# Sliding-window attention and an MLP on one core: which queue brings the first tiles' q and k, how the layer norm's weight arrives, and where the sinks' product is made

## The chip, the cores and the metric

The kernel runs on one core of a Trainium2 chip. The core has a matrix engine (TensorE, PE in the profile; its weight loads are PEld), a vector engine (VectorE, DVE), an activation engine (ScalarE, ACT), a general engine (GpSimd, POOL), a sync engine (SyncE, SP) that issues transfers, and 16 DMA engines that all queues share. SyncE and ScalarE issue transfers to hardware queues. GpSimd issues them to a software queue; in this kernel the loads on it are changed from float32 to bf16 on the way, and those on the hardware queues are not.

The metric is the device time of one execution in microseconds (us), lower is better.

## The reference

Attention with a sliding window of 128 and 4 sink positions over 4 batches, 8 heads, 768 positions and 64 dimensions a head, then a layer norm, a two-layer MLP with ReLU, and a residual:

```python
scores = scale * np.matmul(q, k.transpose(0, 1, 3, 2))
keep = (pos[None, :] < n_sink) | ((rel >= 0) & (rel < window))   # rel = query - key
a = softmax(np.where(keep, scores, -1e9))
x = np.matmul(a, v)                       # heads side by side: [4, 768, 512]
xn = (x - mean) / np.sqrt(var + 1e-6) * g_ln
out = x + np.maximum(xn @ w_ch1, 0.0) @ w_ch2     # 512 -> 2048 -> 512
```

All inputs and the output are float32 in memory.

## The kernel before, in words

The 3072 rows (4 batches of 768) are cut into 24 tiles of 128 rows, and these into 12 chunks of two tiles. For a tile, q, k and v are brought in as 128 rows by 8 heads by 64, in bf16. q and k are transposed, so that the head dimension lies on the partitions. TensorE makes the scores of a tile with itself and with the tile before. ScalarE takes the exponential, a mask is applied, and TensorE multiplies with v, to which a column of ones is appended so that the softmax's sum comes out as a 65th column. From the third tile of a batch on, the four sink positions are outside the window; their part comes from `kts` (the sinks' k) and `vs` (the sinks' v, laid out by head). VectorE divides (L793, L795), and takes the layer norm's mean and variance (L799, L801); x minus its mean is transposed on TensorE (L816) and multiplied with the layer norm's weight `gt` on the way out of PSUM (L827). GpSimd makes the inverse standard deviation (L808, L809). The MLP's first layer is L849 (L842 for the first chunk, which goes tile by tile), ReLU is L859 or L861, the second layer L878, the residual L886, the store L890. The first-layer weights `w1` come in four loads of 512 columns (L520), the second-layer weights `w2` in four loads of 512 rows (L523).

Nothing here is in the order of the program text. Each piece of work is given to a planner (`Plan.op`) with the engines that can do it, an estimate of its duration, a priority (lower goes first), and what it reads and writes. `Plan.run` plays the schedule through with these estimates, also for the transfers, and fixes for each engine the order of its work. Every engine then works through its own list in order; a piece that waits for its input holds up all that stands behind it in that list. `nb` is a time before which the planner does not start a piece. `HW_F`, `SW`, `SW_W` and the like are the planner's figures for a transfer (its occupation of the DMA engines, the time before it and the time after it). Where the planner sees a hole in TensorE's list in the first 24 us, the program fills it with matmuls on a tile of zeros (L944). Transfers from GpSimd's queue rotate over eight semaphores, so that the ninth waits until the first has landed; the hardware queues have eight likewise.

The start, which the change touches:

- Chunk 0 (tiles 0 and 1): k comes by SyncE's queue and q by ScalarE's, in float32, each as two loads of 256 KB (four heads by 256 rows, L570). Two neighbouring rows go to one partition, so that each piece is 512 bytes long. Each load is cast to bf16 (L574, on ScalarE or VectorE), and transposed by four matmuls with an identity, whose results are interleaved as float32 in PSUM (L582), and copied out (L553).
- Chunk 1 (tiles 2 and 3): k and q come by GpSimd's queue with the cast, one load a tile (L599), and are transposed by L604 and copied out as bf16 (L553). v comes by GpSimd's queue for all tiles (L547).
- GpSimd's list begins with two selects that make the identity and the triangle (L458, L461). Then come k2, v0, q2, v1, k3, q3, the first w1 load, v2, v3, three w1 loads, and the loads of chunk 2 and of w2.
- `gt` is one load on SyncE's queue that gathers 512 single float32 values (L504). `vc`, the sinks' v, is eight small loads on SyncE's queue (L508). `vs` of batch 0 is made from it on VectorE (L512), not before 12 us in the plan.
- The masks that are multiplied into the exponentials of tile 3 and later (L479, L480) are built on VectorE at about 3.7 us; tiles 0 to 2 get their mask by a matmul that adds a large negative number (L671).

Of the kernel before, what the change touches and what calls it, by code (L numbers as in the profile page):

```python
# [211 lines left out]
def fix(occ, extra=0.09):  # L212
# [5 lines left out]
HW_F = (0.8, 2.2, 0.5)  # L218
# [10 lines left out]
           w1p=(1.6, 2.6, 2.7, 2.8), pm=3, w2p=(4.5, 4.51, 4.52, 4.53), apart=2, by_tile=1, vp=(0.0, 0.1, 2.0, 2.1, 4.55, 4.56), ld1=0.05)  # L229
# [135 lines left out]
def kernel(  # L365
# [43 lines left out]
    ring("natc", 4, [128, 2, 4, 64], BF16)  # L409
# [24 lines left out]
    gt = const("gt", [128, NDM], FP32)  # L434
# [14 lines left out]

    def constant(name, eng, us, prio, emit, reads=(), **kw):  # L450
        return P.op(name, {eng: fix(us)}, prio, emit, reads=[Bc[r] for r in reads], **kw)
# [6 lines left out]
    constant("idf1", "POOL", 0.3, -99, lambda e: G.affine_select(  # L458
        out=ident_f, in_=ident_f, compare_op=ALU.not_equal, fill=1.0, base=0,
        pattern=[[-1, 128]], channel_multiplier=1), rw=[Bc["ident_f"]])  # L460
    constant("up1", "POOL", 0.3, -98, lambda e: G.affine_select(  # L461
# [27 lines left out]
    def negs(e):  # L489
# [3 lines left out]
    constant("negs", "DVE", 0.9, -55, negs, ["upper"], writes=[Bc["neg"]])  # L493
# [8 lines left out]
    constant("masks", "DVE", 0.8, 6.0 if PAR["pm"] == 4 else -20.0, masks, ["upper"], writes=[Bc["mask"]], nb=20.0 if PAR["pm"] == 4 else 0.0)  # L502

    P.op("gt", {"SP": (0.4, 0.4)}, 3.0, lambda e: nc.sync.dma_start(gt, moe_g_ln.rearrange("(j p) -> p j", p=128)),  # L504
         writes=[Bc["gt"]], dma=HW_T)
    for h in range(H):
        p0 = 32 * (h // 2) + NS * (h % 2)
        P.op(f"vcd{h}", {"SP": (0.3, 0.3)}, 3.2 + 0.01 * h, lambda e, h=h, p0=p0: nc.sync.dma_start(  # L508
            vc[p0:p0 + NS, :, 0:64], v[:, h, 0:NS, :].rearrange("b s d -> s b d")),
            reads=[Bc["vc"]], writes=[Bc["vcd"]], dma=HW_T)  # L510
    for b in range(B):
        P.op(f"vs{b}", {"DVE": dve(520)}, 2.0 if b == 0 else 48.0 * b - 20, lambda e, b=b: V.tensor_tensor(  # L512
            vs[b], vc[:, b, :].unsqueeze(1).to_broadcast([128, H, 65]),
            sel.unsqueeze(2).to_broadcast([128, H, 65]), op=ALU.mult),
            reads=[Bc["vcd"], Bc["vc"], Bc["sel"]], writes=[Bvs[b]], nb=12.0 if b == 0 else 40.0 * b)

    w1prio = PAR["w1p"]
    for c in range(4):
        sl = slice(512 * c, 512 * (c + 1))
        P.op(f"w1ld{c}", {"POOL": (0.75, 0.8)}, w1prio[c], lambda e, c=c, sl=sl: G.dma_start(  # L520
# [15 lines left out]

    def early(t):
        return 0.5 + 0.8 * t
# [17 lines left out]
    def chunk(c):  # L556
# [3 lines left out]
        if c < 2:  # L560
            kT_b[c], qT_b[c] = Buf(f"kT{c}", "kT"), Buf(f"qT{c}", "qT")
            if c == 0:
                nats = [Buf("kf", "natf"), Buf("qf", "natf")]
                for hh in range(2):
                    hs = slice(4 * hh, 4 * hh + 4)
                    for i, (x, T) in enumerate(((k, kT_b[c]), (q, qT_b[c]))):
                        nm, src, part = "kq"[i], nats[i], Buf(f"{'kq'[i]}l{hh}")
                        ap = x[b, hs, 0:256, :].rearrange("h (p i) d -> p h (i d)", i=2)
                        P.op(f"{nm}ld{hh}", {("SP" if i == 0 else "ACT"): (0.53, 0.53)}, -70 + hh,
                             lambda e, src=src, ap=ap, hs=hs: (nc.sync if e == "SP" else nc.scalar).dma_start(  # L570
                                 src.t[:, hs].rearrange("p h i d -> p h (i d)"), ap), writes=[src, part], dma=HW_F)
                        nat, pt, done = Buf(f"{nm}c{hh}", "natc"), Buf(f"pt{nm}{hh}", "one"), Buf(f"{nm}T0{hh}")
                        P.op(f"cast{nm}{hh}", {"DVE": dve(512), "ACT": act(512)}, d + 0.01 * hh,
                             lambda e, nat=nat, src=src, hs=hs: (nc.scalar.copy if e == "ACT" else V.tensor_copy)(  # L574
                                 nat.t, src.t[:, hs].rearrange("p h i d -> p i h d")),
                             reads=[part], hold=[src], writes=[nat])

                        def tr(e, pt=pt, nat=nat):
                            pb = pt.t.rearrange("p (h m i) -> p h m i", h=2, i=2)
                            for hp in range(2):  # L580
                                for i in range(2):
                                    nc.tensor.matmul(pb[:, hp, :, i], lhsT=nat.t[:, i, 2 * hp:2 * hp + 2, :], rhs=ident,  # L582
                                                     start=hp + i == 0, stop=True, skip_group_check=True)
                        o = P.op(f"tr{nm}{hh}", pe(0.3), d + 0.02 + 0.01 * hh, tr, reads=[nat, Bc["ident"]], hold=[T], writes=[pt])
                        trs[0], trs[1] = trs.get(0, [o]), [o]
                        evict(f"ev{nm}0{hh}", d + 0.05 + 0.01 * hh, 512,
                              lambda pt=pt: pt.t.rearrange("p (h c) -> p h c", h=2),
                              lambda T=T, hh=hh: T.t[:, 2 * hh:2 * hh + 2, :], [pt], [T, done], fp=True)
                        for t in range(2):
                            tile_of[nm, t, hh] = done  # L590
# [397 lines left out]
```

## Time and profile before

| what | value |
|---|---|
| runs of the kernel before | 220.88, 221.36, 221.38 us (median 221.36) |
| the profiled execution | 221.36 us, its span 219.9 us |
| TensorE | busy 212.3 us of the span, 2033 matmuls |
| VectorE, ScalarE, GpSimd | busy 118.1, 108.8, 89.5 us |
| GpSimd's queue | 13.11 MB in 74944 packets |
| hardware queues (q1, q10) | 13.93 MB in 33600 packets |

The span runs from the first instruction to the last; the rest of the time lies around it. A line such as L582 is a line of the kernel's text. In a table by stretch each engine's busy time is followed by the number of its instructions in brackets, then come the granted share of TensorE's clock, the DMA engines' busy share and the GB/s moved. In a DMA table a queue's line gives packets, megabytes and the share of 16 engines that its packets took; shares over 100% mean that packets overlap. GpSimd's queue is `q0`, SyncE's and ScalarE's are `q1` and `q10`. "DMA to landing" gives least, median and greatest time from the start of an issue until all of the transfer has arrived.

### The profile page before, as it was taken

How to read it: one execution, taken by the hardware profiler on the slowest of the kernel's cores; microseconds unless marked ns; L12 is line 12 of the kernel's file. 1: busy time of each engine (PE TensorE's matmuls, PEld its weight loads, DVE VectorE, ACT ScalarE, POOL GpSimd, SP SyncE). 2: the span in 40 equal slices, each digit the busy share in tenths (PEclk: the TensorE clock that was granted, in tenths of full speed). 3: DMA queues.
4: the chain of work that ended last, by engine and by line, in shares of the span. 5: the costliest groups of instructions: out<-in, count | busy, mean ns of one | idle time of the engine just before them, and what ended most of it. 6: DMA issues, size and time to landing. Idle time of an engine off the chain costs nothing.

```text
span 219.9 us, 5071 instructions
## 1 busy us (share of the span) xinstructions
PE 212.3 (97%) x2033; PEld 144.7 (66%) x2033; DVE 118.1 (54%) x269; ACT 108.8 (49%) x163; POOL 89.5 (41%) x130
## 2 busy tenths in 40 slices
PE   6898999999999999999999999999999999999993
PEld 2566975764965964964955964964965964965852
DVE  5499745585797735735715815725716715732011
ACT  3776564145546447445546447445546447440610
POOL 7987663798065570760442722740110110120000
PEclk9999999999999999999999999999999999999999
DMA  5999999999999997999999999998723521121103
GB/s 158 158 183 207 176 206 196 155 211 155 162 176 152 138 143 114 148 132 119 143 101 142 127 116 130 135 132 107 124 48 75 125 45 48 48 51 48 48 12 101
DMA packets 108574, 27.44 MB, mean 125 GB/s; under 512 B 99200, under 2 KB 105600, under 8 KB 108544
## 3 DMA queue, kind: packets, MB, share of 16 engines
q0 software_dynamic: 74944, 13.11, 83.1%
q1 hardware_dynamic: 32544, 13.41, 29.4%
q10 hardware_dynamic: 1056, 0.52, 0.9%
q8 instruction: 18, 0.29, 0.6%
q14 instruction: 12, 0.10, 0.1%
HBM read 27.30 MB, written 6.29 MB: 153 GB/s over the span
## 4 chain that ended last, share of the span: by engine, by line
PE 91%; DVE 4%; DMA 2%; ACT 1%; issue 1%; DVEq 0%
PE one L878 39%; PE one L849 35%; PE pair L732 5%; PE pair L780 4%; PE one L842 2%; DMA natf<-in_k_dram 2%; PE pair L775 1%; DVE st L799 1%; PE one L638 1%; DVE x L795 1%; PE one L582 1%; PE one L736 1%; PE pair L671 1%; DVE xnt L827 1%; PE one L816 0%
## 5 line engine op out<-in xcount | busy, mean ns | idle before, releaser
L878 PE MATMUL one<-w,h 128*128 128x512 bf16 (+1 forms) x400 | 89.0, 371 | 0.0
L859 ACT ACTIVATE h<-one 128x512 bf16<-128x512 f32 x95 | 56.8, 598 | 59.5 <-PE one L849 54.2
L849 PE MATMUL one<-xnt,w 128*128 128x256 bf16 x704 | 82.4, 273 | 0.0
L849 PEld LDWEIGHTS <-w 128*128 128x128 bf16 x704 | 67.5, 98 | 10.1
L878 PEld LDWEIGHTS <-h 128*128 128x128 bf16 x400 | 37.4, 98 | 38.6 <-issue 2.1
L750 DVE TENSOR_TENSOR pe<-pe,mask 128x1024 bf16<-128x1024 bf16 (+1 forms) x40 | 26.0, 649 | 54.5 <-ACT pe L746 53.6
L746 ACT ACTIVATE pe<-pair 128x1024 bf16<-128x1024 f32 (+1 forms) x40 | 36.2, 957 | 34.1 <-PE pair L732 34.1
L624 POOL DMA_DIRECT2D nat<-in_k_dram x16 | 14.2, 891 | 37.8 <-DMA kT<-nat 24.3
L886 DVE SCALAR_TENSOR_TENSOR ot<-one,st,x 128x512 f32<-128x512 f32 (+1 forms) x25 | 18.1, 726 | 15.3 <-PE one L878 15.2
L808 POOL TENSOR_SCALAR st<-st 128x1 f32<-128x1 f32 x24 | 6.9, 289 | 42.5 <-DVE st L801 41.3
L547 POOL DMA_DIRECT2D vn<-in_v_dram x24 | 21.9, 916 | 3.7 <-DMA w<-in_moe_w_ch_dram 3.0
L624 POOL DMA_DIRECT2D nat<-in_q_dram x16 | 14.6, 913 | 13.4 <-DMA qT<-nat 12.0
L799 DVE BATCH_NORM_STATS2 st<-x 128x6 f32<-128x512 bf16 x24 | 16.7, 694 | 0.8
L809 POOL TENSOR_TENSOR st<-st,mhalf 128x1 f32<-128x1 f32 x24 | 14.8, 618 | 2.0
L780 PEld LDWEIGHTS <-pe 128*128 128x128 bf16 x352 | 14.0, 97 | 2.2 <-ACT pe L691 0.6
L795 DVE TENSOR_TENSOR x<-pair,rec 128x512 bf16<-128x512 f32 x20 | 13.8, 691 | 0.7
L732 PEld LDWEIGHTS <-kT 64*128 64x128 bf16 x216 | 6.9, 94 | 8.5 <-issue 8.3
L780 PE MATMUL pair<-vn,pe 128*128 128x65 bf16 x296 | 12.2, 193 | 0.0
L732 PE MATMUL pair<-qT,kT 64*128 64x128 bf16 (+1 forms) x216 | 11.6, 238 | 0.0
L803 DVE TENSOR_SCALAR xc<-x,st 128x512 bf16<-128x512 bf16 x24 | 9.6, 402 | 0.9
L793 DVE RECIPROCAL rec<-pair 128x8 f32<-128x8 f32 x20 | 4.0, 200 | 9.9 <-PE pair L780 9.9
L691 ACT ACTIVATE pe<-pair 128x1024 bf16<-128x1024 f32 (+1 forms) x8 | 7.2, 918 | 3.3 <-PE pair L685 3.3
(84 smaller groups left out, 123.9 us busy)
## 6 DMA issues: line engine op xcount, KB each, us to landing
out_dram<-ot SPq DMA_DIRECT2D x23, 256.0 KB
w<-in_moe_w_ch_dram POOLq DMA_DIRECT2D x8, 512.0 KB, 12.8
vn<-in_v_dram POOLq DMA_DIRECT2D x24, 128.0 KB, 6.4
nat<-in_k_dram POOLq DMA_DIRECT2D x22, 128.0 KB, 5.8
nat<-in_q_dram POOLq DMA_DIRECT2D x22, 128.0 KB, 5.3
natf<-in_q_dram ACTq DMA_DIRECT2D x2, 256.0 KB
natf<-in_k_dram SPq DMA_DIRECT2D x2, 256.0 KB
xnt<-xc SPq DMA_TRANSPOSE x18
```

The costliest lines, as they stand in the source:

```text
L547: P.op(f"vld{t}", {"POOL": (0.87, 0.9)}, prio, lambda e: G.dma_start(bv.t[:, :, 0:64], v[b, :, 128 * r:128 * (r + 1), :].rearrange("h p d ...
L624: lambda e, nat=nat, ap=ap: G.dma_start(nat.t, ap), writes=[nat], dma=SW)
L732: nc.tensor.matmul(pp.t[:, h2, col:col + q1 - q0], lhsT=kt.t[rs, hp, k0:k0 + 128], rhs=qT.t[rs, hp, q0:q1], start=i == 0, stop=True, skip_ ...
L746: P.op(f"ex{c}{hp}", {"ACT": act(2 * n)}, d + 0.1 + 0.05 * j, lambda e, pp=pp, pb=pb: nc.scalar.activation(pb.t[:, :, 0:n], pp.t[:, :, 0:n ...
L750: V.tensor_mul(pb.t[:, :, 0:n], pb.t[:, :, 0:n], mm),
L780: nc.tensor.matmul(bank(h // 4)[:, 65 * (h % 4):65 * (h % 4) + 65], lhsT=part(h, n), rhs=vn_b[tv].t[:, h, :], start=(not R and h % 4 == 0 ...
L795: P.op(f"x{t}{run[0]}", {"DVE": dve(512 * share)}, dd + 0.11, lambda e, pv=pv, rc=rc, run=run: V.tensor_tensor(x.t[:, 256 * run[0]:256 * r ...
L799: P.op(f"bn{t}", {"DVE": fix(0.60)}, d + 0.12, lambda e: V.bn_stats(st.t[:, 8:14], x.t), reads=[x], writes=[st, mv])
L849: nc.tensor.matmul(ph.t[:, 256 * s:256 * s + 256], lhsT=w1[ht // 4][:, j, 128 * (ht % 4):128 * (ht % 4 + 1)], rhs=xnt.t[:, j, :], start=j ...
L859: nc.scalar.activation(hb.t, ph.t, AF.Relu)
L878: nc.tensor.matmul(pc.t[:, 0:wd], lhsT=(h1[2 * s + i].t[:, 128 * ii:128 * ii + 128] if by_tile else h1[ht // 2].t[:, 256 * (ht % 2) + 128 ...
L886: V.scalar_tensor_tensor(ot.t[:, sl], in0=pc.t[:, 0:wd], scalar=st.t[:, 16:17], in1=x.t[:, sl], op0=ALU.mult, op1=ALU.add),
```

## The change

- Of the first tiles' q and k, only k of tile 0 still comes by the hardware queues: 128 rows in two loads of 128 KB, heads 0 to 3 by SyncE's queue, heads 4 to 7 by ScalarE's, each cast in a piece of 256 elements. q of tile 0, and k and q of tile 1, come by GpSimd's queue with the cast, as those of tiles 2 and 3 do. All four tiles are transposed in the same way, four transposes an operand into bf16 in PSUM. The ring `natc` goes.
- GpSimd's work at the start gets priorities by one list, `front`: q0, the identity, the triangle, k1, q1, v0, v1, k2, q2, the first w1 load, v2, k3, q3, v3, `vs` of batch 0, and the three other w1 loads.
- `vs` of batch 0 is made on GpSimd. Those of the other batches stay on VectorE.
- The layer norm's weight comes as four rows of 128 values, is transposed by TensorE, and copied to `gt` by VectorE.
- The multiplied masks are built not before 5.4 us in the plan. The planner's figures for the first hardware loads, for the sinks' small loads and for the transposes change.

```diff
-HW_F = (0.8, 2.2, 0.5)
+HW_F = (0.5, 0.8, 0.7)
...
-           w1p=(1.6, 2.6, 2.7, 2.8), pm=3, w2p=(4.5, 4.51, 4.52, 4.53), apart=2, by_tile=1, vp=(0.0, 0.1, 2.0, 2.1, 4.55, 4.56), ld1=0.05)
+           pm=3, w2p=(4.5, 4.51, 4.52, 4.53), apart=2, nbs=(0.0, 5.4), by_tile=1, hw=("k0",),
+           front=("q0", "ident", "upper", "k1", "q1", "v0", "v1", "k2", "q2", "w0", "v2", "k3", "q3", "v3", "vs", "w1", "w2", "w3"))
...
+    def early(t):
+        return 0.5 + 0.8 * t
+
+    def front(name):
+        return -110.0 + 0.1 * PAR["front"].index(name)
...
-    constant("idf1", "POOL", 0.3, -99, lambda e: G.affine_select(
+    constant("idf1", "POOL", 0.3, front("ident"), lambda e: G.affine_select(
...
-    constant("masks", "DVE", 0.8, 6.0 if PAR["pm"] == 4 else -20.0, masks, ["upper"], writes=[Bc["mask"]], nb=20.0 if PAR["pm"] == 4 else 0.0)
-
-    P.op("gt", {"SP": (0.4, 0.4)}, 3.0, lambda e: nc.sync.dma_start(gt, moe_g_ln.rearrange("(j p) -> p j", p=128)),
-         writes=[Bc["gt"]], dma=HW_T)
+    constant("masks", "DVE", 0.8, 6.0 if PAR["pm"] == 4 else -20.0, masks, ["upper"], writes=[Bc["mask"]], nb=20.0 if PAR["pm"] == 4 else PAR["nbs"][1])
+
+    g_rows, ptg = Buf("g_rows"), Buf("ptg", "one")
+    P.op("gtld", {"SP": (0.4, 0.4)}, 3.0, lambda e: nc.sync.dma_start(g4, moe_g_ln.rearrange("(j p) -> j p", p=128)),
+         writes=[g_rows], dma=HW_T)
+    P.op("gttr", pe(0.1), early(0) + 0.3, lambda e: nc.tensor.transpose(ptg.t[:, 0:NDM], g4, ident_f[0:NDM, 0:NDM]),
+         reads=[g_rows, Bc["ident_f"]], writes=[ptg])
+    P.op("gtev", {"DVE": fix(0.08)}, early(0) + 0.5, lambda e: V.tensor_copy(gt, ptg.t[:, 0:NDM]), reads=[ptg], writes=[Bc["gt"]])
...
-        P.op(f"vs{b}", {"DVE": dve(520)}, 2.0 if b == 0 else 48.0 * b - 20, lambda e, b=b: V.tensor_tensor(
+        P.op(f"vs{b}", {"DVE": dve(520)} if b else {"POOL": (0.9, 1.0)}, front("vs") if b == 0 else 48.0 * b - 20, lambda e, b=b: (V if b else G).tensor_tensor(
...
-        P.op(f"w1ld{c}", {"POOL": (0.75, 0.8)}, w1prio[c], lambda e, c=c, sl=sl: G.dma_start(
+        P.op(f"w1ld{c}", {"POOL": (0.75, 0.8)}, front(f"w{c}"), lambda e, c=c, sl=sl: G.dma_start(
...
+            for t in (2 * c, 2 * c + 1):
                 d, at_t = early(t), slice(128 * (t % 2), 128 * (t % 2) + 128)
+                shared = Buf(f"pt{t}", "one") if c else None
+                for i, (x, T) in enumerate(((k, kT_b[c]), (q, qT_b[c]))):
+                    nm, nat = f"{'kq'[i]}{t}", Buf(f"{'kq'[i]}n{t}", "nat")
+                    ap = x[b, :, 128 * t:128 * t + 128, :].rearrange("h p d -> p h d")
+                    if nm in PAR["hw"]:
+                        src = Buf(f"{nm}f", "natf")
...
                         for hh in range(2):
+                            hs, part = slice(4 * hh, 4 * hh + 4), Buf(f"{nm}l{hh}")
+                            P.op(f"{nm}ld{hh}", {("SP", "ACT")[hh]: (0.5, 0.5)}, -70 + i,
+                                 lambda e, raw=raw, ap=ap, hs=hs: (nc.sync if e == "SP" else nc.scalar).dma_start(
+                                     raw()[:, hs], ap[:, hs]), writes=[src, part], dma=HW_F)
...
+                    else:
+                        P.op(f"{nm}ld", {"POOL": (0.87, 0.9)}, front(nm), lambda e, nat=nat, ap=ap: G.dma_start(nat.t, ap),
+                             writes=[nat], dma=SW)
```

## The prediction

> **What bounds the kernel now.** I read the page's busy shares first, then the busy time by stretch, the chain of waits of the first 30 us, and last the loads. All times are microseconds from the start of the span.
>
> ```profile
> PE 212.3 (97%) x2033; PEld 144.7 (66%) x2033; DVE 118.1 (54%) x269; ACT 108.8 (49%) x163; POOL 89.5 (41%) x130
> ...
> 5.46:8.00 2.54, 2.47 (x20) 1.66 (x21) 0.90 (x2) 2.05 (x4) 2.54 (x4) 1.00 1.77 162
> 8.00:12.00 4.00, 3.50 (x53) 2.31 (x52) 2.65 (x8) 2.64 (x5) 4.00 (x6) 1.00 2.32 159
> 12.00:16.00 4.00, 3.67 (x56) 2.27 (x54) 3.79 (x10) 3.11 (x5) 3.15 (x6) 1.00 1.71 186
> 16.00:20.00 4.00, 3.50 (x68) 2.80 (x65) 3.79 (x11) 2.95 (x7) 3.04 (x5) 1.00 1.31 206
> 20.00:22.60 2.60, 2.08 (x40) 1.72 (x38) 2.53 (x7) 1.36 (x3) 2.03 (x3) 1.00 1.24 207
> 42.00:216.00 174.00, 174.00 (x1584) 118.56 (x1580) 90.82 (x190) 84.57 (x126) 59.78 (x87) 1.00 1.06 112
> ```
>
> After the stretch come its length, then the busy time of PE, PEld, DVE, ACT and POOL. From 42 to 216 TensorE is never idle at a granted clock of 1.00: nothing in this change can shorten that part. TensorE's loss is 5.46 us before its first useful matmul, and 0.07 + 0.50 + 0.33 + 0.50 + 0.52 = 1.9 us of gaps up to 22.6. What the change can win or lose is there.
>
> ```profile
> 1.02 3.75 DMA natf<-in_k_dram
> 4.79 0.63 ACT natc L574
> ...
> 12.30 0.70 DVE st L799
> ...
> 16.68 0.70 DVE vs L512
> ...
> 22.82 2.68 PE one L842 x48
> ```
>
> The chain (start, length, what): the first k load, its cast, ACT's exponentials, then VectorE from 11 to 21 (busy 3.79 of 4 us), the sinks' product at 16.68 among it; from 21.6 TensorE itself.
>
> ```profile
> q10 hardware_dynamic: 857, 0.43, 66.7%
> q1 hardware_dynamic: 722, 0.33, 50.0%
> ...
> q0 software_dynamic: 1681, 0.21, 166.8%
> ...
> DMA to landing us min/median/max: 6.2/6.3/6.5
> ...
> DMA to landing us min/median/max: 8.0/11.0/13.7
> ...
> DMA to landing us min/median/max: 3.5/6.4/13.4
> ```
>
> The first two lines are all the DMA traffic of 3.6 to 6.0, and the third is GpSimd's queue from 6 to 8: its first load, issued at 1.86, moves nothing until the hardware queues' 1 MB is through. The landings are those of the tile 2 and 3 loads (L599), of w1 (L520), and of v (L547). The four w1 loads are issued at 7.36 and 9.84 to 12.1; the first lands at 7.36 + 8.0 = 15.4, and TensorE's first L842 starts at 15.43; the last, issued at 11.33, lands 13.7 later, at 25.0, and the L842 group that needs it starts at 25.56. So two things bound the front together: VectorE's chain, and a stream of loads that arrives 0.1 to 0.6 us before its use.
>
> **The change part by part.** The profiled execution took 221.36 us, of which 219.9 is the span; it is itself the median of the runs, so the sum is made against 221.36. 0.3% of it, 0.66 us, is about what a measurement tells from no change.
>
> Hardware queues: 1 MB in four loads becomes 256 KB in two, half on SP, half on ACT, both issued at 1.02. The old first half (256 KB) landed 3.75 later. By 3.6 some 0.25 MB had moved, as much as there is now in all; so the new halves land between 3.6 and 4.8. The casts go from four of 512 elements (615 ns on ACT, 448 on VectorE) to two of half that, side by side, about 0.3 us: first useful matmul at 4.1 to 5.2 rather than 5.46.
>
> GpSimd's queue: three loads (q0, k1, q1) are added at 0.9 us of issue each (L599: 0.92 to 1.10). By the new order q0 goes ahead of the two mask selects (0.29 us each), from 1.05 to 2.15. These then end near 2.65 rather than 1.9. That is hidden: their first reader is the transpose of k0 at 4.1. If the cover were gone it would cost 0.75. After them follow k1, q1, v0, v1, k2, q2, the first w1, v2, k3, q3, v3, the sinks' product, and the other w1. With 0.91 each, q2 is issued at 7.2, the first w1 at 8.1, v3 at 11.6.
>
> When do they land? An undisturbed load of this kind lands 3.5 after its issue (least of L547); behind 1 MB it took 6.5. With a quarter of the hardware traffic I take q0 near the first: 1.05 + 3.6 = 4.7, other end 7.55. The last w1, two ways: from q0's landing, the old stream took from k2's landing at 1.86 + 6.5 = 8.4 to 25.0, that is 16.6, for seven small and four large loads; three more small ones at 0.89 give 4.7 + 19.3 = 24.0. By issue, q2 lands at 7.2 + 3.5 = 10.7, and the old spacings (2.56 for w1, 0.98 for each of four small, 7.67 for three w1) give 24.8. I take 24.5: half a microsecond earlier than 25.0 although three loads were added, because the stream starts when it is issued and not at 6.2.
>
> [...]
>
> Transposes: sixteen L582 matmuls at 0.45 to 0.61 us a group of four become sixteen like L604, 0.39 a group. That takes off 0.2 to 0.8 of TensorE time and turns float evictions (0.59 to 0.69) into bf16 ones (0.42 to 0.58). It helps only where TensorE doesn't wait for a load.
>
> Sinks' product: VectorE loses 0.70 that stood on the chain at 16.68. On GpSimd its price isn't in the trace. By rows it lies between 0.7 (VectorE's own) and 1.8 (a 128 element select of 0.29, times 4.06, times the 1.5 by which L809 grew from 0.57 to 0.86 beside a busy VectorE); I take 1.2, by the select. It waits for the eight sink loads, the last of which should be issued near 6.3; even 6.3 us later (L599) they are there at 12.6, about when v3's issue ends. The three w1 are queued behind it; issued at 13.8 rather than 12.5, they still meet a stream busy until 16 to 16.6, so 0. The cover ends when the product ends after 14.7, from where each microsecond costs one. [...]
>
> LN weight: 512 elements of 4 bytes become four rows, a transpose (0.1, as one of L816) and a copy (0.2, as L793 on a small operand). The transpose stands early in TensorE's order, and what lies behind it waits if the rows are late. Their load is issued at 1.5; they come between 3.75 (the first k) and 6.3 (L599) later, at 5.3 to 7.8. I take 5.3, since they follow only k0 on their queue. At 7.8 tile 0 would lose up to 2.5, of which the wait for the first w1 (13.0) still hides most, since tile 0 is otherwise ready near 12.5. Building the masks later (0.32 + 0.27) moves into a VectorE that is busy 1.08 of 4 us there: 0, or 0.6 of the same slack.
>
> Tiles 0 to 3: tile 0's value product moves from 10.5 to about 8.2 (v0 is issued at 4.5 and lands near 8.0), tile 1 with it. k3 and q3 land at 15 to 16 instead of 12 to 13, still ahead of tile 3's old scores at 18.2. So VectorE's chain runs 1 to 3 us ahead and leaves the bound to the loads.
>
> Sum at the last w1, where both kernels meet: landing 0.5 earlier, the 0.56 of slack before its use gone as well, and one second-chunk unit (0.87, L849) that may now run before it, counted at 0.15: 1.2 us. From there on the loads keep their 0.5 lead and TensorE is full. 221.36 - 1.2 = **220.2 us**; its own range, from 0.2 to 0.9 of lead and none or one unit, is 219.5 to 220.7.
>
> **The rivals.** (1) The transfers come no earlier: the added loads use up the earlier start, and the last w1 stays at 25.0. Only slack is won, 0.5: 220.9 (220.7 to 221.5). For it: the bytes are the same and the packets shorter; against it, the undisturbed landing of 3.5.
>
> (2) Slower: GpSimd's first load starts 4.3 after its issue whatever else runs, as k2 did (1.86 to 6.2). Then q0 lands at 7.55 and the last w1 at 7.55 + 19.3 = 26.9, 1.9 later; less 0.56 of slack and none or one unit of 0.87, TensorE loses 0.5 to 1.4: 221.9 to 222.8. It decides once q0 lands after about 6.5. Against it: the hardware queues' traffic ends at the moment GpSimd's begins.
>
> (3) Slower by the sinks' product: it ends after 14.7 and holds three w1 back; ending at 17 it costs 2.3 less 1.1: 222.5.
>
> (4) More is won: TensorE fills the wait for the last w1 with one or two units and saves the 0.8 of transposes: 2.1 to 2.7, so 218.7 to 219.3.
>
> **How the numbers follow.** Forecast 0.47, rival 1 0.20, rival 2 0.15, rival 3 0.08, rival 4 0.10. Below 220.7 lie the forecast but 0.02, rival 4, and 0.04 of rival 1: 0.59. Above 222.02 lie 0.13 of rival 2 and rival 3: 0.21. Between: 0.20. The range 219.2 to 222.5 leaves out most of rival 4 and the upper ends of 2 and 3, together 0.19.
>
> **What would show it.** Right: GpSimd's first packets before 4, q0's landing 3.5 to 4 after issue, the first L842 near 13, the last w1 landing at 24 to 24.8, first useful matmul at or before 5.2, no VectorE product at 16.68. Wrong: packets of GpSimd's queue first at 5 or later, TensorE waiting for the transposed weight, the product ending after 14.7, or gaps of TensorE after 26 that before did not have.

## The result, and the profile after

The changed kernel is slower. Its six runs took 222.68 to 225.07 us, median 223.92; six runs of the kernel before on the same chip took 220.88 to 221.85, median 221.38. The ratio is 1.0099, 95% interval 1.0076 to 1.0123. The profiled execution took 223.05 us with a span of 221.4, so 1.7 us more than the one before; it is one of the quicker of the six. The forecast was 220.2, with a range of 219.2 to 222.5: wrong in sign, and outside the range.

First the busy shares of the changed kernel's page, and its busy time by the same stretches as before (PE, PEld, DVE, ACT, POOL, then the granted clock, the DMA share, GB/s):

```profile
PE 209.6 (95%) x2012; PEld 143.8 (65%) x2032; DVE 116.1 (52%) x267; ACT 108.7 (49%) x163; POOL 92.3 (42%) x134
...
5.46:8.00 2.54, 1.62 (x18) 0.88 (x18) 1.64 (x7) 1.29 (x3) 2.54 (x4) 1.00 1.94 126
8.00:12.00 4.00, 3.08 (x44) 1.69 (x44) 2.72 (x9) 2.11 (x3) 4.00 (x6) 1.00 2.02 146
12.00:16.00 4.00, 2.98 (x48) 1.98 (x49) 3.34 (x9) 2.79 (x6) 3.99 (x5) 1.00 1.76 172
16.00:20.00 4.00, 3.54 (x66) 3.09 (x63) 2.85 (x8) 2.61 (x5) 3.81 (x6) 1.00 1.72 190
20.00:22.60 2.60, 2.35 (x41) 1.73 (x38) 1.70 (x4) 2.26 (x4) 1.39 (x3) 1.00 1.24 208
42.00:216.00 174.00, 172.42 (x1573) 118.53 (x1590) 91.57 (x191) 84.57 (x126) 60.42 (x88) 1.00 1.07 113
```

From 42 to 216 TensorE is as dense as before (20 fewer matmuls than weight loads are in the records of the page, so a few matmuls are missing from it, not from the work). The loss lies ahead of that. VectorE, which was busy 3.79 of 4 us from 12 to 20, now has 3.34 and 2.85: it is no longer the bound. TensorE has more gaps than before from 5.46 to 16 (7.68 of 10.54 us busy, before 9.64). So VectorE and TensorE both wait, and the next view says for what. It is the chain of waits of the first 36 us (start, length, what):

```profile
1.57 1.08 POOL nat L586
...
2.76 0.31 POOL ident_f L464
3.06 0.24 POOL upper L467
3.31 1.74 POOL nat L586 x2
...
6.79 1.75 POOL nat L586 x2
8.54 0.75 POOL w L529
...
12.83 1.01 POOL vs L522
13.84 7.63 DMA w<-in_moe_w_ch_dram
...
21.75 13.87 DMA w<-in_moe_w_ch_dram
35.66 1.89 PE one L868 x8
```

Before, this chain went over VectorE and TensorE. Now it is GpSimd's list of issues, one behind the other almost without a hole, and then two loads of weights: the second w1 load, which lands at 21.46, and a load of w2 whose issue waits for that landing (21.75) and which lands at 35.6. TensorE's list shows the same from the other side. Of its first-layer units (L832, the L842 of before) the first, the third and the seventh, which is the first that reads the last w1, each start on a load of w1:

```profile
15.58 1.07 PE L832 MATMUL one<-xnt,w 128*128 128x128 bf16 x16 [0.63 <-DMA w<-in_moe_w_ch_dram]
...
21.51 1.07 PE L832 MATMUL one<-xnt,w 128*128 128x128 bf16 x16 [0.25 <-DMA w<-in_moe_w_ch_dram]
...
26.62 1.57 PE L832 MATMUL one<-xnt,w 128*128 128x128 bf16 x25 [0.26 <-DMA w<-in_moe_w_ch_dram]
```

Before, the unit on the last w1 started half a microsecond after that load had landed, without a wait:

```profile
25.56 1.95 PE L842 MATMUL one<-xnt,w 128*128 128x128 bf16 x32
```

Now it starts at 26.62, 0.04 after the landing. A smaller loss follows at the load of w2: the second group of second-layer matmuls starts at 35.66, when that load has landed, and 1.4 later than before, where it ran through:

```profile
34.29 1.90 PE L878 MATMUL one<-w,h 128*128 128x512 bf16 x8
```

The two answers on w1 and on the loads of q and k give the landings:

```profile
L529 POOL DMA_DIRECT2D w<-in_moe_w_ch_dram x4: 750/784/815, 8.5 to 15.4; - x4
...
DMA to landing us min/median/max: 7.0/8.5/11.2
```

```profile
L586 POOL DMA_DIRECT2D nat<-in_q_dram x4: 881/937/1088, 1.6 to 11.0; - x4
L586 POOL DMA_DIRECT2D nat<-in_k_dram x3: 913/913/945, 3.3 to 10.1; - x3
...
DMA to landing us min/median/max: 4.1/4.4/7.1
```

The last w1 is issued at 15.38 and lands 11.2 later, at 26.58 (before 25.00); the first lands at 15.53 (15.36). The first q loads land 4.1 to 4.4 after their issue: far sooner than the 6.2 of before, and slower than the 3.5 that the forecast took.

### The profile page after: what moved, and what is told of

The parts are those of the page before. It is cut to its first block, busy times and chain, and to the rows that moved or that the text cites. A ratio compares the mean times of both kernels' runs of the same rounds, so it can differ in the third digit from the quotient of the medians.

```text
span 221.4 us, 5059 instructions
## 1 busy us (share of the span) xinstructions
PE 209.6 (95%) x2012; PEld 143.8 (65%) x2032; DVE 116.1 (52%) x267; ACT 108.7 (49%) x163; POOL 92.3 (42%) x134
## 3 DMA queue, kind: packets, MB, share of 16 engines
HBM read 27.30 MB, written 6.29 MB: 152 GB/s over the span
## 4 chain that ended last, share of the span: by engine, by line
PE 81%; DMA 10%; POOL 5%; issue 2%; DVE 0%; POOLq 0%; DVEq 0%
PE one L868 37%; PE one L839 34%; DMA w<-in_moe_w_ch_dram 10%; PE pair L722 4%; PE pair L770 4%; POOL nat L586 3%; PE pair L765 1%; POOL vn L553 1%; PE one L726 1%; POOL vs L522 0%; PE one L628 0%; POOL w L529 0%; DVE ot L876 0%; PE one L806 0%; POOL ident_f L464 0%
## 5 line engine op out<-in xcount | busy, mean ns | idle before, releaser
L868 PE MATMUL one<-w,h 128*128 128x512 bf16 (+1 forms) x380 | 86.9, 370 | 1.8 <-issue 0.9
L736 ACT ACTIVATE pe<-pair 128x1024 bf16<-128x1024 f32 (+1 forms) x40 | 36.2, 957 | 34.2 <-PE pair L722 34.2
L876 DVE SCALAR_TENSOR_TENSOR ot<-one,st,x 128x512 f32<-128x512 f32 (+1 forms) x25 | 18.1, 726 | 15.7 <-PE one L868 15.6
L614 POOL DMA_DIRECT2D nat<-in_q_dram x16 | 14.7, 919 | 11.3 <-DMA qT<-nat 9.1
L799 POOL TENSOR_TENSOR st<-st,mhalf 128x1 f32<-128x1 f32 x24 | 14.0, 582 | 2.0
L785 DVE TENSOR_TENSOR x<-pair,rec 128x512 bf16<-128x512 f32 x20 | 13.8, 691 | 0.7
L793 DVE TENSOR_SCALAR xc<-x,st 128x512 bf16<-128x512 bf16 x24 | 9.1, 381 | 0.9
L832 PE MATMUL one<-xnt,w 128*128 128x128 bf16 x128 | 8.0, 219 | 1.1 <-DMA w<-in_moe_w_ch_dram 1.1
```

Source lines behind the costliest of these rows:

```text
L614: lambda e, nat=nat, ap=ap: G.dma_start(nat.t, ap), writes=[nat], dma=SW)
L736: P.op(f"ex{c}{hp}", {"ACT": act(2 * n)}, d + 0.1 + 0.05 * j, lambda e, pp=pp, pb=pb: nc.scalar.activation(pb.t[:, :, 0:n], pp.t[:, :, 0:n ...
L799: G.tensor_tensor(st.t[:, 16:17], st.t[:, 17:18], mhalf, op=ALU.pow)),
L868: nc.tensor.matmul(pc.t[:, 0:wd], lhsT=(h1[2 * s + i].t[:, 128 * ii:128 * ii + 128] if by_tile else h1[ht // 2].t[:, 256 * (ht % 2) + 128 ...
L876: V.scalar_tensor_tensor(ot.t[:, sl], in0=pc.t[:, 0:wd], scalar=st.t[:, 16:17], in1=x.t[:, sl], op0=ALU.mult, op1=ALU.add),
```

## The experiments

One reading ties all profiles of this study together, so it comes first. A unit is the 16 matmuls of a first-layer line for one tile and one load of w1. The table gives for each kernel the landing of the first and of the last w1, the start of the first unit that reads the last one (its first weight load), and the time of the same execution.

| kernel | first w1 | last w1 | unit starts | time | time less start |
|---|---|---|---|---|---|
| before | 15.36 | 25.00 | 25.51 | 221.36 | 195.9 |
| after | 15.53 | 26.58 | 26.62 | 223.05 | 196.4 |
| e1_after_again | 16.35 | 28.47 | 29.49 | 225.38 | 195.9 |
| e2_hw4 | 14.38 | 25.74 | 27.94 | 223.99 | 196.1 |
| e3_rest | 15.16 | 24.77 | 25.52 | 221.21 | 195.7 |
| e4_loads | 17.21 | 28.23 | 28.27 | 224.25 | 196.0 |
| e5_hw2 | 15.21 | 26.23 | 26.27 | 222.21 | 195.9 |
| e6_w0 | 14.32 | 29.20 | 29.24 | 224.78 | 195.5 |
| e7_sel | 15.61 | 26.64 | 27.08 | 223.71 | 196.6 |
| e8_hold | 16.87 | 28.75 | 29.84 | 225.55 | 195.7 |
| e9_vs | 15.44 | 25.13 | 25.53 | 221.50 | 196.0 |
| e10_gt | 15.16 | 24.94 | 26.63 | 222.12 | 195.5 |
| e11_late_w | 15.45 | 25.35 | 26.56 | 222.75 | 196.2 |
| e12_rest_again | 15.24 | 25.05 | 25.53 | 221.24 | 195.7 |

What follows that unit takes 195.5 to 196.6 us in every one of them, though its start moves over 4.3 us. So the whole question is what holds this unit up. In after, e4, e5 and e6 it starts 0.04 after the last w1 has landed: the load holds it. In before, e3, e9 and e12 it starts 0.4 to 0.8 after it, when TensorE is through with what stands ahead. In e1, e2, e7, e8, e10 and e11 it is 0.4 to 2.2: in these executions TensorE had half its clock for some microseconds (e1, e2, e7, e8) or started slowly (e1, e8, e10, e11), which is told below.

### Which part of the change costs the time

The changed kernel unaltered, on another chip and beside the next runs:

> The changed kernel unaltered, for a second profile. Theory A (the stream of loads on GpSimd's queue ends later and sets the time): the last w1 lands at 26.3 to 27.3 and the time is 222.7 to 225.1; where this execution is slower than the first profiled one (223.05), the last w1 or the w2 loads land later by as much. Theory B (the other parts, the sinks' product on GpSimd and the transposed weight, or a worse order on TensorE, carry the loss): the extra time appears as gaps of TensorE that no load ends.

Measured 224.25 us (223.49 to 225.38), ratio 1.0112 [1.0088, 1.0136]. The loss is the kernel's, not one chip's. The profiled execution is the slowest of the six; its last w1 lands at 28.47, later than the 26.3 to 27.3 expected, and why that landing differs by 1.9 us between two executions of one kernel is taken up below.

The loads alone: the changed kernel with the sinks' product back on VectorE and the weight as one gather.

```diff
-        P.op(f"vs{b}", {"DVE": dve(520)} if b else {"POOL": (0.9, 1.0)}, front("vs") if b == 0 else 48.0 * b - 20, ...
+        P.op(f"vs{b}", {"DVE": dve(520)}, 2.0 if b == 0 else 48.0 * b - 20, ...
...
-    P.op("gtld", ... g4, moe_g_ln.rearrange("(j p) -> j p", p=128)) ... "gttr" ... "gtev"
+    P.op("gt", {"SP": (0.4, 0.4)}, 3.0, lambda e: nc.sync.dma_start(gt, moe_g_ln.rearrange("(j p) -> p j", p=128)),
```

> The changed kernel with the sinks' product back on VectorE and the weight gathered by one load as before; loads and GpSimd's order as changed. Theory A: last w1 at 26.2 to 27.0, time 222.7 to 224.5 as the changed kernel. Theory B: 221.0 to 222.0.

Measured 223.76 us (223.17 to 224.28), ratio 1.0089 [1.0070, 1.0108]: nearly the whole loss, within the noise. Its last w1 landed at 28.23, again later than expected (26.2 to 27.0).

The rest alone: the kernel before with the weight as four rows, and the sinks' product on GpSimd behind the second w1 (the planner's figures for the sinks' loads change with it).

```diff
-        P.op(f"vs{b}", {"DVE": dve(520)}, 2.0 if b == 0 else 48.0 * b - 20, ...
+        P.op(f"vs{b}", {"DVE": dve(520)} if b else {"POOL": (0.9, 1.0)}, 2.65 if b == 0 else 48.0 * b - 20, ...
...
-    P.op("gt", {"SP": (0.4, 0.4)}, 3.0, ...
+    P.op("gtld", {"SP": (0.4, 0.4)}, 3.0, ... g4, moe_g_ln.rearrange("(j p) -> j p", p=128)) ...
+    P.op("gttr", pe(0.1), 0.8, lambda e: nc.tensor.transpose(ptg.t[:, 0:NDM], g4, ident_f[0:NDM, 0:NDM]), ...
+    P.op("gtev", {"DVE": fix(0.08)}, 1.0, lambda e: V.tensor_copy(gt, ptg.t[:, 0:NDM]), ...
```

> The kernel before, with only the sinks' product on GpSimd (behind v3's issue's place, ahead of the later w1 loads) and the weight as four rows; all loads as before. Theory A: last w1 at 24.8 to 25.3, time 220.6 to 221.6. Theory B: 222.5 or more.

Measured 221.11 us (220.57 to 221.83) against 221.67, ratio 0.9974 [0.9961, 0.9988]. Without the moved loads the other two parts gain a quarter of a per cent; this beats both kernels. So the loss belongs to what e4 keeps: the moved loads of q and k, with the order of GpSimd's list and the later masks that go with them. The next two kernels take loads back and leave that order.

### How many loads by which queue

Three loads taken back: q of tile 0 and k and q of tile 1 come by the hardware queues again, in halves like k of tile 0, into a second ring of buffers (the priorities of these loads, not shown, now go by tile).

```diff
-           hw=("k0",),
+           hw=("k0", "q0", "k1", "q1"),
...
+    ring("natg", 2, [128, H, 1, 64], FP32)
...
-                        src = Buf(f"{nm}f", "natf")
+                        src = Buf(f"{nm}f", "natg" if t else "natf")
```

> The changed kernel, but q0, k1 and q1 also come by the hardware queues (eight loads of 128 KB in float32, each cast); the sinks' product stays on GpSimd, the weight in rows, the new order of GpSimd's list. Theory A: GpSimd's queue has its old eight small loads before the last w1, which lands at 24.7 to 25.5, and the time falls to 220.9 to 222.0. Theory B: the time stays above 222.7.

Measured 222.05 us (221.71 to 223.99), ratio 1.0022 [1.0009, 1.0035]: 2.2 of e1's 2.6 us are back, so most of the loss is the loads'. The median and the last w1 (25.74) lie just above the ranges expected. What remains is of two kinds. On GpSimd's list (start, length, what, and in brackets the idle time before it) the sinks' product waits for the sink loads:

```profile
14.98 1.06 POOL L523 TENSOR_TENSOR vs<-vc,sel 128x520 bf16<-128x520 f32 x1 [3.76 <-DMA vc<-in_v_dram]
15.99 1.55 POOL L530 DMA_DIRECT2D w<-in_moe_w_ch_dram  x2
```

It ends at 16.0 and holds the last two w1 until then: the prediction's third rival, seen here and not in the changed kernel. The second kind is the clock. In the profiled execution, by stretch:

```profile
5.00:8.40 3.40, 2.11 (x22) 0.93 (x20) 1.86 (x5) 3.03 (x7) 3.40 (x5) 1.00 1.73 184
8.40:11.80 3.40, 2.89 (x20) 1.76 (x20) 1.35 (x4) 0.61 (x2) 2.22 (x3) 0.50 1.92 177
11.80:15.30 3.50, 3.50 (x36) 1.91 (x34) 3.03 (x10) 2.26 (x3) 0.32 (x1) 0.51 1.97 170
```

After 3.4 us in which TensorE was busy for 2.11 (before: 3.26 in the same stretch), it is granted half its clock for 6.8 us. The three of its 13 runs with a mean clock of 0.99 or less took 222.57, 223.10 and 223.99; the ten others took 221.71 to 222.46.

One load taken back, q of tile 0:

```diff
-           hw=("k0",),
+           hw=("k0", "q0"),
```

> The changed kernel, but q0 comes by the hardware queues like k0, so that two loads instead of three are added to GpSimd's queue. If each added load costs the same, a third of what e2 gained (2.2 us of 224.25) comes back: 223.2 to 223.8, last w1 0.7 to 1.0 earlier than in the changed kernel (25.6 to 27.5). If the loss hangs on GpSimd's queue being first at work with q0, and not on the number of loads, nearly all comes back: 222.3 or less.

Measured 222.34 us (221.38 to 223.69), ratio 1.0034 [1.0013, 1.0054]. One load is a third of what was moved, and by the ratios it gives back some 1.7 of the 2.5 us, where a third (223.2 to 223.8) was expected if each load costs the same. How much it really gives back is uncertain: of its twelve runs, in the order of the record, the first six took 221.38 to 222.21 us and the last six 222.46 to 223.69, with mean clocks of 0.997 or more in all, so the median lies between two groups. In the profiled execution, one of the first six, the last w1 lands at 26.23, only 0.35 earlier than in the changed kernel. GpSimd now starts with the selects, as before the change, and issues its first load at 1.86 and the first w1 at 7.35 rather than 8.49.

### Does GpSimd's time of issue pass on?

The two selects ahead of q0 again, so that the issues behind them have no hole:

```diff
-           front=("q0", "ident", "upper", "k1", ...
+           front=("ident", "upper", "q0", "k1", ...
```

> The changed kernel with the two mask selects ahead of q0 on GpSimd, as the kernel before has them. By the pace of issues: k1 is issued at 2.95 instead of 3.25 and all behind it 0.3 earlier, q0 0.3 later; last w1 0 to 0.4 earlier, time 223.5 to 224.4. By the bytes: 0 to 0.3 later, since q0's transfer starts later. A small effect is expected either way.

Measured 224.15 us (223.60 to 224.51), ratio 1.0111 [1.0090, 1.0132]. k1 is issued at 2.95 rather than 3.25, the first w1 at 8.16 rather than 8.49. The 0.3 us is not seen in the time (e1: 1.0112), and the last w1 of the profiled execution lands at 26.64. The order of the selects is not what costs.

The other direction: an unused product of 128 by 520 on GpSimd ahead of k1. Nothing of the output depends on it.

```diff
+    spare = const("spare", [128, H, 65], BF16)
+    constant("spare", "POOL", 1.0, front("upper") + 0.05, lambda e: G.tensor_tensor(
+        spare, ident_f[:, 0:65].unsqueeze(1).to_broadcast([128, H, 65]), ...
```

> The changed kernel with a product of 128 by 520 on GpSimd whose result nobody reads (1.1 us), between the selects and k1's issue. If GpSimd's issues pace the stream until the first w1, all of it passes on: the first w1 and the last w1 land 0.8 to 1.1 later, time 224.8 to 225.6. If the bytes pace it, the last w1 moves by less than 0.4 and the time by less than 0.4.

Measured 225.08 us (224.18 to 225.78), ratio 1.0147 [1.0122, 1.0172]. k1 is issued at 4.27, about 1.0 later than in the changed kernel, and the time rises by 0.8 over e1 (225.08 - 224.25). So by the time, the later issues cost most of their delay, as expected; the issues that came a little earlier in e7 gained nothing that can be seen. The landings don't decide it: the last w1 lands at 28.75, 2.2 later than in the first profile of the changed kernel but 0.3 later than in e1.

### The first w1

In the changed kernel's trace the packets of the first w1 start slowly. A packet of w1 usually takes 97 to 98 ns; between 10.7 and 13.5 us some take up to 635 ns, in e1 up to 1158. In e1 this shows in the GB/s of the single microseconds (in the changed kernel's own profile the same two have 170 and 184):

```profile
11.00:12.00 1.00, 1.00 (x10) 0.25 (x6) 0.93 (x4) 0.57 (x1) 1.00 (x3) 1.00 1.07 92
12.00:13.00 1.00, 1.00 (x13) 0.52 (x13) 0.93 (x3) 0.52 (x2) 1.00 (x2) 1.00 1.11 154
```

and in e3, with the loads of before, where the first w1 comes at the same time:

```profile
11.00:12.00 1.00, 1.00 (x18) 0.61 (x16) 0.31 (x2) 0.34 (x1) 0.00 (x0) 1.00 1.70 188
12.00:13.00 1.00, 1.00 (x18) 0.58 (x14) 0.93 (x4) 0.88 (x1) 0.01 (x1) 1.00 1.27 207
```

The slow packets were there in each profile in which the first w1's packets began 1.4 to 1.8 us after the end of its issue (after, e1, e4 to e8), and not where they began 3.0 to 3.7 us after it (before, e2, e3). Two kernels try this. In the first the first w1 is moved ahead in GpSimd's list:

```diff
-           front=(... "k1", "q1", "v0", "v1", "k2", "q2", "w0", "v2", ...
+           front=(... "k1", "q1", "v0", "w0", "v1", "k2", "q2", "v2", ...
```

> The changed kernel with the first w1 load moved ahead in GpSimd's list, behind v0 instead of behind q2; the same loads in another order. If the pace of GpSimd's issues holds the stream back (a large load gives GpSimd 1.7 us of lead), the last w1 lands 0.4 to 1.0 earlier and the time falls by 0.3 to 1.0, to 223.2 to 223.9. If the bytes alone hold it, nothing changes (223.7 to 224.7). And if the slow packets of the first w1 (up to 1.2 us each, at 10.7 to 14 us in the three profiles with these loads) belong to a time, they hit other loads now; if to the first w1, they move to about 8 to 10.

Measured 223.88 us (223.41 to 224.78), ratio 1.0094 [1.0074, 1.0114]. The slow packets moved with the load, to 8.2 to 11.4. They go with the first w1 and not with a time. The first w1 lands 1.2 us earlier, the last 2.6 later in the profiled execution, which is the slowest of the six. The median, that of the changed kernel, lies in both of the ranges expected, so the time does not decide between pace and bytes; the earlier landing of the last w1 that pace would bring did not come.

In the second, two unused products on GpSimd hold up the first w1's issue in the kernel before (nothing of the output depends on them):

```diff
+    spare = const("spare", [128, H, 65], BF16)
+    for n in range(2):
+        constant(f"spare{n}", "POOL", 1.0, 1.59, lambda e: G.tensor_tensor(
+            spare, ident_f[:, 0:65].unsqueeze(1).to_broadcast([128, H, 65]), ...
```

> The kernel before with two products of 128 by 520 on GpSimd whose results nobody reads (2.2 us), ahead of the first w1 load's issue: its issue moves from 7.36 to about 9.5, while the stream is busy with q3 until 11.2 either way. If the slow packets of the first w1 come from its standing in the queue for 2 us or less, they appear here too (packets over 250 ns before 15), the first w1 lands at 15.7 to 16.8 and the last at 25.3 to 26.5, time 221.9 to 223.2. If not, no packet over 250 ns, the first w1 lands near 15.4, and the time is 221.5 to 221.9.

Measured 222.55 us (222.22 to 222.94), ratio 1.0032 [1.0017, 1.0047]. Here is the stretch in which its first w1 starts:

```profile
10.00:11.00 1.00, 0.68 (x12) 0.42 (x9) 0.71 (x4) 0.89 (x1) 1.00 (x2) 1.00 2.44 155
11.00:12.00 1.00, 0.82 (x12) 0.52 (x13) 0.32 (x2) 0.62 (x2) 1.00 (x2) 1.00 1.96 131
```

The issue ends at 10.41 rather than 8.12, its first packets run 1.1 us after that, and slow packets of up to 693 ns appear from 11.5 on, in a kernel that had none. So moving that issue alone (with the work on GpSimd that moves it) brings the slow packets, as the waits of 1.8 and 3 us said. Its price is not: the first w1 lands 2.73 after the load ahead of it, against 2.56 in the kernel before, so 0.17, where the changed kernel lost 0.96. The 0.7 us of the median is not explained by it either, because this execution also had TensorE late from the start (below).

### The part that gains

Each part of e3 alone, in the kernel before: the sinks' product on GpSimd, and the weight as rows. The edits are those shown at e3.

> The kernel before with only the sinks' product on GpSimd, between the second and the third w1 load. VectorE loses 0.70 us that stood on the chain at 16.68. If that is what made e3 faster (221.11 against 221.67), this one is 221.0 to 221.4; if the weight's rows did it, 221.5 to 221.9.

> The kernel before with only the layer norm's weight as four rows. 512 single values of 4 bytes leave the hardware queues, so GpSimd's first packets come 0.2 to 0.4 earlier. If the weight made e3 faster, 221.0 to 221.4; if the sinks' product did, 221.5 to 221.9.

Measured 221.65 us (221.14 to 222.22), ratio 1.0001 [0.9987, 1.0014], and 221.92 us (221.45 to 222.43), ratio 1.0008 [0.9995, 1.0021]. Neither gains clear of the noise by itself. So both together were run again on another chip:

> The same kernel as the one with the loads of before and both other parts of the change (weight rows, sinks' product on GpSimd). The parts alone came out at 1.0001 and 1.0008 of before, both together at 0.9974. If the two together really win (the sinks' product out of VectorE's row and the weight rows on a shorter queue), the ratio is 0.9974 again, within 0.996 to 0.999. If that was chance of one chip, it lies within 0.999 to 1.002, as the sum of the two parts alone (1.0009) says.

Measured 221.15 us (220.71 to 221.66) against 221.67, ratio 0.9975 [0.9961, 0.9989]. The gain is there twice. Its cause isn't settled. In e3 and e12 the third first-layer unit starts at 20.21 and 20.22 rather than 21.39, because VectorE no longer makes the product at 16.68, but the unit on the last w1 starts at 25.52 and 25.53, as in before (25.51), and the profiled executions differ by only 0.15 us where the medians differ by 0.5. e9 has the same early third unit (20.14) without the gain.

## Why the prediction was wrong

**The step that failed** is "When do they land?", with its "I take 24.5". Its sum by issue, "q2 lands at 7.2 + 3.5 = 10.7", and from there by the old spacings to 24.8, can be laid beside the trace term by term:

| term | forecast | measured | difference |
|---|---|---|---|
| q2's issue | 7.2 | 7.62 | +0.4 |
| q2 from issue to landing | 3.5 | 4.4 | +0.9 |
| from there to the first w1 | 2.56 | 3.52 | +1.0 |
| from there to the last w1 | 11.59 | 11.05 | -0.5 |
| last w1 lands | 24.8 | 26.58 | +1.7 |

The 0.4 is the list: GpSimd starts its first issue at 1.57 and not at 1.05, after a wait that the profile puts down to its own queue, and the selects end at 3.31 and not near 2.65. The 0.9 is the term with the wrong idea in it. The forecast took the shortest landing of a load in the trace of before (3.5) and the spacing of loads in a queue that had a backlog (0.89), and used both for a queue in which the loads follow each other at the pace of their issue. (A load into an empty queue did land as fast: in e8, where the unused product holds k1 back, 3.4 after its issue.) This is what the DMA engines moved from 4 to 10 us, nearly all of it for GpSimd's queue:

```profile
4.00:5.00 1.00, 1.00 (x7) 0.33 (x5) 0.42 (x5) 0.56 (x2) 1.00 (x2) 1.00 1.60 107
5.00:6.00 1.00, 0.41 (x6) 0.33 (x6) 0.95 (x4) 0.00 (x0) 1.00 (x3) 1.00 1.32 90
6.00:7.00 1.00, 0.76 (x12) 0.35 (x11) 0.96 (x4) 0.59 (x1) 1.00 (x2) 1.00 1.87 123
7.00:8.00 1.00, 0.66 (x12) 0.31 (x8) 0.14 (x1) 0.70 (x2) 1.00 (x2) 1.00 2.13 137
8.00:9.00 1.00, 0.57 (x6) 0.34 (x6) 0.42 (x2) 0.39 (x1) 1.00 (x2) 1.00 2.27 145
9.00:10.00 1.00, 0.77 (x16) 0.49 (x16) 0.47 (x2) 0.00 (x0) 1.00 (x2) 1.00 2.02 129
```

The kernel before moved 155 to 157 GB/s in each microsecond from 7.5 to 10.5:

```profile
7.50:8.50 1.00, 0.94 (x10) 0.73 (x10) 0.13 (x2) 0.98 (x3) 1.00 (x2) 1.00 2.37 155
8.50:9.50 1.00, 0.89 (x14) 0.37 (x12) 0.99 (x3) 0.42 (x2) 1.00 (x2) 1.00 2.40 157
9.50:10.50 1.00, 0.61 (x9) 0.38 (x6) 0.80 (x2) 1.00 (x2) 1.00 (x2) 1.00 2.41 155
```

The six stretches of the changed kernel fall short of 156 by 49, 66, 33, 19, 11 and 27, together 205, which is 1.3 us of that stream. GpSimd is busy all the time in them (1.00). It issues such a load in 0.88 to 0.95 us, and the forecast's 0.89 for carrying one off is about the same, so hardly a backlog forms, and the queue moves what GpSimd hands it. That the issue sets this pace is read from these figures and borne out by the time of e8; no run made GpSimd's issue itself faster. e5 fits it: when its queue begins at 4.0, two loads are ready and a third is under way, and it then moves 146, 140, 152, 142 and 130 GB/s from 5 to 10, against 90, 123, 137, 145 and 129 here. In the kernel before, the queue stood still until 6.29, but GpSimd went on issuing: four loads were ready by then and a fifth was under way, and from 7.5 on they drained at the 155 to 157 GB/s above. The earlier start was counted in full, and it is worth less. In sum: first packets at 3.42 rather than 6.29 give 2.9 us; three more loads take 2.7, the shortfall 1.3 and the late landing of the first w1 1.0; 0.5 comes back on the way to the last w1. That is 1.6 later, as measured. The sum is that of this execution, one of the quicker of its kernel. In e1, e4, e6 and e8 the last w1 lands at 28.2 to 29.2.

The 1.0 comes together with the slow packets, but that they make all of it is not shown. Their time beyond 98 ns adds up to 3.4 us, which is 0.2 us on each of sixteen engines if it is spread evenly, and the 170, 184 and 190 GB/s from 11 to 14 against 193, 203 and 193 in before (11.5 to 14.5) are 0.2 us short. The rest is unevenness: when the first w1 had landed, GpSimd's queue had moved 1.66 MB, 0.22 MB more than the loads up to it hold (before: 1.46 MB, 0.15 more), so loads behind it were already being carried while a part of it was missing. The trace doesn't tell which engine carried a packet, so whether slow packets held that part stays open. Nothing in the trace of before showed them, and no rival held them.

**The sum at the last w1** (0.5 of landing, 0.56 of slack, 0.15 for a unit, 1.2 in all) had its mechanism right in the main: the slack did go, and the unit starts 0.04 after the landing. With 26.58 in place of 24.5 the same sum gives a loss of 0.9 us (1.58 of landing, less 0.56 and 0.15); at the unit it is 1.1. That nothing changes behind it did not hold: 1.1 grows to 1.4 at the load of w2 that lands at 35.6, a step that the sum left out, and to 1.5 at the end of the span.

**The second rival** gave the last w1 at 26.9, close to 26.58, and 221.9 to 222.8 us; but not its reason. It had GpSimd's first load start 4.3 us after its issue whatever else runs. The DMA view from 3 to 5 us shows GpSimd's queue at work beside the last of the hardware queues' traffic:

```profile
q0 software_dynamic: 1032, 0.13, 102.1%
q10 hardware_dynamic: 374, 0.09, 20.6%
q1 hardware_dynamic: 162, 0.04, 9.5%
```

Its first packets run at 3.42, 1.85 after the issue began, and q0 lands at 5.75, before the 6.5 that was to decide for this rival. In the kernel before, the first packet ran at 6.29, 4.43 after the issue began, when the hardware queues' 1 MB was nearly through (its last packet starts at 6.42). So between these two kernels the wait shrank with their traffic. e2, with 1 MB on the hardware queues again, speaks against their traffic as the cause: from 5.4 to 7.8 us GpSimd's queue moved 0.14 MB beside 0.31 MB of theirs. So what held GpSimd's queue until 6.29 in the kernel before is not settled.

**The first rival** had the last w1 unchanged at 25.0, and the fourth had more won; both fall with the same line.

**The third rival** did not come about: the product takes 1.08 us (forecast 1.2) and ends at 13.9, ahead of the 14.7 from which it was to cost, and the other three w1 start directly behind v3.

**What was right.** k of tile 0 is cast in 0.7 us from 3.85, and the first useful matmul runs at 4.31 (forecast 4.1 to 5.2, before 5.46). The weight's transposition runs at 4.94 without a wait (rows forecast at 5.3). VectorE's product at 16.68 is gone and VectorE is no longer the bound. The issue of the later w1 was forecast at 13.8 and is at 13.84. **What was not:** tile 0's value product at 9.49 (forecast 8.2), k3 and q3 at 17.2 and 18.1 (15 to 16), the first L832 at 15.58 (near 13). All are late by the loads, and so it did not help that tile 0 started 1.2 us earlier.

The six runs lie up to 2.4 us apart, those of before 1.0. e1's execution shows two of the reasons. Its last w1 lands 1.9 later than in the other profile: 0.8 of it stands already at the first w1, and 1.1 comes until the second, though GpSimd issues that one at the same time (13.73 and 13.84). By that last landing the queue had moved 3.95 MB, 0.41 more than the loads up to it hold (in the other 3.74 MB, 0.20 more), so here too it was carried unevenly. And there is a half clock just where the units on w1 run:

```profile
19.00:23.40 4.40, 2.91 (x48) 2.08 (x45) 3.52 (x9) 3.67 (x6) 2.45 (x3) 1.00 1.27 204
23.40:26.80 3.40, 3.31 (x37) 3.18 (x38) 1.11 (x4) 0.60 (x1) 2.75 (x6) 0.50 1.63 187
```

In it the 16 matmuls of a unit took 1.89 us (from 23.49), where the changed kernel's first profile has 1.07, and the unit on the last w1 starts 1.0 after that load has landed, and not 0.04.

What stays open: how the loads come to land so unevenly, so that one kernel's last w1 moves by 1.9 us between executions; why the packets of a large load are slow when they start soon after its issue, why the first w1 came 1.0 later in one kernel and 0.2 in another; and why e5's runs fall in two groups.

## What to carry to other kernels

Here a queue that stood still until 6.29 lost less than the standstill, since its issuer went on working and the backlog of four loads drained without holes, from 7.5 on at 155 to 157 GB/s; before counting such a standstill as something to win, compare the time to issue a load with the time to carry it off. Here the two are about equal (0.9 us each): the queue that started at 3.42 built hardly any backlog, and with three loads moved onto it the last one landed 1.6 later. Look for the load that is used last and the first work that needs it: in fourteen profiles that one start gave the time to within 0.6 us either way.

## What the runs showed of the hardware that was not expected

In five of the fourteen profiled executions TensorE was granted half its clock right behind a stretch of sparse work. The stretches at half clock that their traces record there are one or two times 3.41 us long (in before and after the full clock stands for 215.04 us, 63 times as long): 0.50 for 6.8 us from 8.4, 8.2 and 8.0 in e2, e4 and e7, and for 3.4 us from 23.4 and 24.2 in e1 and e8. In the 3.41 us right ahead of the loss TensorE was busy for 2.15 (e2), 1.76 (e4), 2.08 (e7), 1.94 (e1) and 1.97 us (e8). Counted from the same record, the sparsest stretches of the first 30 us that kept the clock were busy for 2.26 (the changed kernel, 5.66 to 9.07) and 2.28 us (e5, 11.94 to 15.36); in the kernel before none was under 2.88. So up to there the busy time of these stretches separates loss from none. It does not for 3.4 us laid otherwise (from 5.00 to 8.40 the changed kernel was busy for 1.83 and kept the clock), nor in the whole program: at its end stretches of 1.46 (e8) and 2.04 us (e11) kept the clock. e4 and the changed kernel do nearly the same work from 4.8 to 9.1, and e4's stretch lies 0.9 us earlier (4.8 to 8.2); whether the place of the stretch decides was not tested.

The start can be slow without the clock row showing it. In e10's and e11's executions the first transposes and mask matmuls took 1.6 to 1.7 times as long as in before, and tile 0 was late by 0.9 us from there on. Of e10:

```profile
5.57 1.06 PE L586 MATMUL one<-ident,natc 128*128 128x128 bf16 x4
6.34 1.02 PE L675 MATMUL pair<-neg,ident 128*128 128x512 bf16 x2
```

and of before:

```profile
5.46 0.61 PE L582 MATMUL one<-ident,natc 128*128 128x128 bf16 x4
5.87 0.64 PE L671 MATMUL pair<-neg,ident 128*128 128x512 bf16 x2
```

The clock row reads 1.00 in both. e12, which has the same work up to there as e10, shows 0.61 and 0.64, so it changes from one execution to the next. The row reads 1.00 where the trace holds no record of the clock, and the first record comes at 4.5 to 6.0 us in nine of the profiles, at 7.11 in e10 and e11, and at 13.15, 14.59 and 13.94 in e1, e6 and e8. Ahead of these three late records the matmuls of a group follow each other at 107 ns and not at 56. Here is the first mask matmul pair of e1:

```profile
6.05 1.06 PE L661 MATMUL pair<-neg,ident 128*128 128x512 bf16 x2
```

and of the changed kernel's first profile:

```profile
6.03 0.59 PE L661 MATMUL pair<-neg,ident 128*128 128x512 bf16 x2
```

So of the six profiles in which all three loads come by GpSimd's queue, five ran slowly for 6.8 us or more of the first 15, and the first profile is the exception; of the profiles with the loads of before none ran slowly beyond 7.1. That may be a second way in which the moved loads cost time, since they leave TensorE with sparser work (from 5.00 to 8.40 it was busy for 1.83 us in the changed kernel's first profile, and for 3.26 in before); that the sparser work brings it is not shown. It cost nothing at the unit on the last w1 in e4 and e6, which started 0.04 after the landing; what it cost in runs without a profile isn't shown, as their mean clock doesn't count it (e6's reads 0.999).

Why the start is slow in one execution and not in another was not tested.
